# Sparse attention with a feed-forward block on one core: six early buffers for P, another set of numbers for the planner, and W2 loads and result stores issued by GpSimd

## The chip, the cores and the metric

The kernel runs on one NeuronCore of a Trainium2 chip. The metric is the device time of one execution in microseconds (us). Its engines are named as the profile names them: PE is TensorE (matmuls; PEld its weight loads), DVE is VectorE, ACT is ScalarE, POOL is GpSimd, SP is SyncE, which here only issues DMAs.

## The reference, cut to what matters

```python
# q, k, v: (4, 8, 768, 64) float32; blocks of 32 keys; 24 blocks
scores = (1/8) * q @ k.T
scores = where(mask, scores, -1e9)     # window, first/last block, 3 sampled blocks per query block
attn = exp(scores - max(scores)); attn = attn / (sum(attn) + 1e-9)
x = (attn @ v), heads side by side      # (4, 768, 512)
xn = (x - mean(x)) / sqrt(var(x) + 1e-6) * g_ln
out = x + relu(xn @ w_ch1) @ w_ch2      # 512 -> 2048 -> 512; w_ch1, w_ch2 are float64
```

## The kernel before, in words

The work is cut into 12 **units**, one for each batch and each chunk of 256 queries. A unit has 4 **segments**, one for each pair of heads, and a segment has 4 **slots** (2 tiles of 128 queries times 2 heads), 192 in all. Two slots make a pair, whose scores PE computes side by side, each head on 64 of the 128 rows.

All products are made of float16 halves. A number x is kept as a high part (x rounded to float16) and a low part (what is left), and a product is three matmuls: high times high, high times low, low times high. So queries, keys, values, P and both weight matrices are each split: somebody casts the high part (ACT by a cast, or a casting DMA that POOL issues), and DVE or POOL subtracts the low part.

For a slot PE makes the scores (`scores`, L587), DVE adds the mask and takes the maximum while it moves the scores from PSUM into P (`masked_max`, L596), ACT takes the exponential (L610). The first 9 segments are **early**: their P stays float32, PE transposes it (L625) into banks that ACT copies out (L632), and PE multiplies it with V in float32 (L701). Later segments split P into `ph` (ACT, L662) and `pl` (DVE, L666), and DMA transposes on SP's queue turn them.

After the 4 segments of a unit come the layer norm and the feed-forward block (`ffn`): 8 groups of the first product (FFN1, 24 matmuls each), each followed by ACT's high part `hh` (L883) and DVE's low part `hl` (L889), then the second product (FFN2) and the results `ot` (L905), which are stored to memory in 4 pieces per unit.

The weights come as float64 and are turned into scaled float32 by three integer steps on DVE (`first` L514, `second` L518, then `third` L522, or `third_low` L527 with an addition on POOL, L532, for those listed in `PORC`), cast to the high part on ACT (L556, L558; or by a DMA of POOL, L568, for those that are in both `HIDMA` and `PORC`), and the low part is subtracted by DVE (L564, those in `LOWDVE`) or POOL (L562). W1 comes in 8 pieces of 1 MB, W2 in 16 pieces of 0.5 MB. Their raw data use places that other data need as well: `raw0`, `raw1` (which the keys share) and unused parts of the weights' own tiles.

What sets the order is `Plan`: a list of tasks, each with an engine, a cost, tasks before it, a rank and buffers that it takes and gives back. `plan.run()` walks through them once when the program is built, picks on each engine the ready task with the earliest start, ties broken by rank, and emits instructions in this order. All engines then execute their own lists strictly in order, and wait only where data or buffers ask for it. So the numbers at the head of the function (ranks such as `W1AT`, `W2AT`, `AVAT`, `MASKAT`, offsets such as `EVAC`, `EXPO`) decide the order of every engine's list. Where the planner finds a hole on PE before `KEEP` nanoseconds, it puts in **filler** matmuls (L294), which compute nothing that is used.

Of the kernel before, what the change touches and what calls it, by code (L numbers as in the profile page):

```python
# [10 lines left out]
F16 = mybir.dt.float16  # L11
# [165 lines left out]
def sparse_attention_moe(  # L177
# [12 lines left out]
    nc = tc.nc  # L190
# [24 lines left out]
    SPLITAT = 7.38  # L215
    VDVE = 1
    KDVE, QDVE = 3, 1
    HIDMA = ((1, 5), (2, 15), (2, 2), (1, 7), (2, 5), (2, 4))
    LEAD = 2.8
    HIGHAT, LOWAT = -0.42, -1.36  # L220
    EVAC, EXPO = -9.12, 1.22
    PLAIN = 'full'
    LOWDVE = ((2, 12), (1, 3), (2, 2), (1, 6), (1, 1), (2, 8), (2, 11), (1, 7), (2, 4), (2, 15), (2, 6), (2, 3), (1, 0), (2, 13), (2, 5))
    AVHOLD = 4
    KEEP = 40000.0
    CASTK, CASTQ = 5, 6
    MASKAT = 25.07
    KAT, VAT, QAT = 11.39, 7.48, 12.65
    AVAT = -17.05
    W1AT = (8.87, 9.4, 10.72, 12.06, 12.3, 15.45, 16.92, 18.19)  # L230
    W2AT = (10.6, 14.04, 14.21, 15.7, 17.12, 20.44, 21.31, 22.16, 23.71, 24.25, 25.32, 25.67, 25.7, 25.75, 26.19, 28.74)
# [5 lines left out]
    pp = ctx.enter_context(tc.tile_pool(name="pp", bufs=2))  # L237
# [11 lines left out]

    plan = Plan()  # L250
# [33 lines left out]
    ql_s = [const.tile([P, CH], F16, name=f"ql{i}") for i in range(NQ)]  # L284
    w1h = const.tile([P, CT, DF], F16, name="w1h")
# [54 lines left out]
    def loads_k(b, pr, rank, before):  # L340
        idx = b * NPAIR + pr
        o = SimpleNamespace()

        def raw():
# [3 lines left out]
            nc.sync.dma_start(o.kr, ks[b, pr])  # L348
# [4 lines left out]
        o.raw = plan.add("SP", 580, raw, (before,), rank, 2000, load=1120, order="k",  # L353
# [773 lines left out]
```

## Time and profile before

| | |
|---|---|
| time, median of 3 runs | 793.22 us (792.82 to 796.02) |
| the profiled execution | 792.63 us, of which the span from first to last instruction is 790.9 us |
| granted TensorE clock | 0.999 of full speed |
| PE busy | 777.9 us (98%) |
| PEld, DVE, ACT, POOL busy | 599.3, 615.4, 498.3, 130.4 us |

The span is the time from the first to the last instruction of the profiled execution; the 1.7 us beside it lie before and after. A busy share is an average over the span.

### The profile page before, as it was taken

How to read it: one execution, taken by the hardware profiler on the slowest of the kernel's cores; microseconds unless marked ns; L12 is line 12 of the kernel's file. 1: busy time of each engine (PE TensorE's matmuls, PEld its weight loads, DVE VectorE, ACT ScalarE, POOL GpSimd, SP SyncE). 2: the span in 40 equal slices, each digit the busy share in tenths (PEclk: the TensorE clock that was granted, in tenths of full speed). 3: DMA queues.
4: the chain of work that ended last, by engine and by line, in shares of the span. 5: the costliest groups of instructions: out<-in, count | busy, mean ns of one | idle time of the engine just before them, and what ended most of it. 6: DMA issues, size and time to landing. Idle time of an engine off the chain costs nothing.

```text
span 790.9 us, 18452 instructions
## 1 busy us (share of the span) xinstructions
PE 777.9 (98%) x7327; PEld 599.3 (76%) x7327; DVE 615.4 (78%) x1216; ACT 498.3 (63%) x935; POOL 130.4 (16%) x140
## 2 busy tenths in 40 slices
PE   8999999999999999999999999999999999999998
PEld 5556677778777777777777777777777877778887
DVE  7999999979888778879877978778877878874220
ACT  6789776567676566667666667567656656652110
POOL 1343542321101002220101102120001100000000
PEclk9999999999999999999999999999999999999999
DMA  9463537998777567999667778997866755570000
GB/s 331 163 194 118 152 106 152 199 213 162 166 129 135 126 129 146 188 196 155 159 123 127 135 137 150 186 190 161 160 105 125 154 115 114 123 136 18 21 1 27
DMA packets 286694, 111.24 MB, mean 141 GB/s; under 512 B 253968, under 2 KB 278416, under 8 KB 286608
## 3 DMA queue, kind: packets, MB, share of 16 engines
q1 hardware_dynamic: 278544, 104.91, 61.2%
q0 software_dynamic: 7776, 5.05, 5.5%
q8 instruction: 57, 0.93, 0.5%
q14 instruction: 29, 0.24, 0.1%
q10 hardware_dynamic: 288, 0.10, 0.1%
HBM read 47.16 MB, written 6.29 MB: 68 GB/s over the span
## 4 chain that ended last, share of the span: by engine, by line
PE 88%; DVE 5%; ACT 3%; DMA 3%; issue 0%; ACTq 0%; DVEq 0%
PE bank L302 61%; PE ps L587 12%; PE pa L705 7%; PE pa L710 3%; PE pa L701 2%; PE bank L625 2%; DMA pt<-pl 2%; DVE p L596 1%; ACT p L610 1%; ACT pt L632 1%; DVE pl L666 1%; DVE allow L317 0%; DMA allow<-blocks 0%; PE pa L726 0%; PE bank L782 0%
## 5 line engine op out<-in xcount | busy, mean ns | idle before, releaser
L302 PE MATMUL bank<-hh,w2h 128*128 128x256 f16 x768 | 204.6, 273 | 0.0
L302 PE MATMUL bank<-hh,w2l 128*128 128x256 f16 x768 | 204.2, 273 | 0.0
L302 PE MATMUL bank<-hl,w2h 128*128 128x256 f16 x768 | 204.2, 273 | 0.0
L596 DVE CUSTOM_DVE_ANT_1 p<-ps,allow 128x768 f32<-128x768 f32 x192 | 178.1, 950 | 22.9 <-PE ps L587 22.6
L610 ACT ACTIVATE p<-p,st 128x768 f32<-128x768 f32 x192 | 178.4, 931 | 18.5 <-DVE st L596 18.2
L662 ACT ACTIVATE ph<-p,st 128x768 f16<-128x768 f32 x156 | 140.4, 927 | 59.6 <-DVE st L653 20.7
L666 DVE SCALAR_TENSOR_TENSOR pl<-p,st,ph 128x768 f16<-128x768 f32 x156 | 160.1, 1040 | 10.5 <-DMA pt<-pl 10.5
L302 PEld LDWEIGHTS <-w2h 128*128 128x128 f16 x1536 | 146.7, 98 | 27.0 <-issue 10.5
L302 PEld LDWEIGHTS <-w1h 128*128 128x128 f16 x1536 | 147.8, 98 | 25.5 <-issue 8.8
L302 PE MATMUL bank<-xh,w1h 128*128 128x256 f16 x768 | 115.4, 273 | 1.0 <-ACT pt L632 1.0
L302 PE MATMUL bank<-xh,w1l 128*128 128x256 f16 x768 | 115.4, 273 | 0.0
L302 PE MATMUL bank<-xl,w1h 128*128 128x256 f16 x768 | 115.4, 273 | 0.0
L889 DVE SCALAR_TENSOR_TENSOR hl<-bank,hh 128x512 f16<-128x512 f32 x96 | 66.1, 688 | 53.9 <-ACT hh L883 53.2
L883 ACT ACTIVATE hh<-bank 128x512 f16<-128x512 f32 x96 | 56.8, 591 | 75.3 <-PE bank L302 74.7
L302 PEld LDWEIGHTS <-w1l 128*128 128x128 f16 x768 | 73.8, 98 | 12.4 <-issue 4.1
L302 PEld LDWEIGHTS <-w2l 128*128 128x128 f16 x768 | 75.0, 98 | 9.1 <-issue 0.3
L705 PE MATMUL pa<-pt,vh 128*64 128x512 f16 x468 | 80.0, 383 | 0.9 <-DMA pt<-pl 0.9
L384 POOL DMA_DIRECT2D qh<-q x42 | 24.3, 579 | 277.7 <-PE ps L587 277.6
L587 PE MATMUL ps<-kh,qh 64*128 64x256 f16 (+1 forms) x384 | 66.0, 328 | 1.2 <-DVE st L596 1.1
L387 POOL TENSOR_TENSOR ql<-qr,qh 128x256 f16<-128x256 f32 x47 | 43.9, 935 | 139.9 <-DMA qr<-q 77.3
L587 PE MATMUL ps<-kl,qh 64*128 64x256 f16 (+1 forms) x384 | 64.4, 323 | 1.6 <-DVE kl L351 1.6
L587 PEld LDWEIGHTS <-qh 64*128 64x128 f16 x768 | 30.9, 94 | 45.8 <-issue 23.5
(110 smaller groups left out, 906.7 us busy)
## 6 DMA issues: line engine op xcount, KB each, us to landing
qr<-q SPq DMA_DIRECT2D x48, 128.0 KB, 2.8
raw<-k SPq DMA_DIRECT2D x16, 384.0 KB, 4.6
raw<-w SPq DMA_DIRECT2D x12, 512.0 KB, 3.9
vr<-v SPq DMA_DIRECT2D x32, 192.0 KB, 2.8
out<-ot SPq DMA_DIRECT2D x48, 128.0 KB, 1.9
w2l<-w SPq DMA_DIRECT2D x4, 1024.0 KB, 8.1
qh<-q POOLq DMA_DIRECT2D x42, 64.0 KB, 2.8
pt<-ph SPq DMA_TRANSPOSE x156, 2.7
```

What stands on the lines that cost most here:

```text
L302: nc.tensor.matmul(dst, w, x, start=start, stop=stop, skip_group_check=True)
L384: o.high = plan.add("POOL", 560, lambda: nc.gpsimd.dma_start(o.qh, qs[u.b, pr, u.c]), (o.raw,), rank, 2300, load=400, order="q")
L387: o.low = plan.add(e, x, lambda: (nc.vector if n < QDVE else nc.gpsimd).tensor_sub(o.ql, o.qr, o.qh), (o.raw, o.high), rank, give=(("qr", ...
L587: nc.tensor.matmul(s.ps[:, lo:hi], x[rows, s.qs], y[rows, lo:hi], start=n == 0, stop=n == len(terms) - 1)
L596: nc.vector.tensor_tensor_reduce(out=s.p.rearrange(blk, k=BLK), in0=s.ps[:, 0:S].rearrange(blk, k=BLK), in1=bias, scale=-0.125, scalar=3.0 ...
L610: nc.scalar.activation(s.p, s.p, AF.Exp, bias=s.st[:, j : j + 1], scale=-1.0, accum_out=total)
L662: nc.scalar.activation(s.ph, s.p, AF.Copy, scale=s.r)
L666: nc.vector.scalar_tensor_tensor(out=s.pl, in0=s.p, scalar=s.r, in1=s.ph, op0=ALU.mult, op1=ALU.subtract)
L705: nc.tensor.matmul(seg.pa[half[hh], 0 : 2 * CH], vo.vh[:, hh, t, :], pts[keys[hh]][:, t].rearrange("p i n -> p (i n)"), start=t == 0, stop ...
L710: nc.tensor.matmul(seg.pa[half[hh], 0:CH], vo.vl[:, hh, t, :], pts[keys[hh]][:, t, 0, :], start=False, stop=t == KT - 1, skip_group_check= ...
L883: nc.scalar.activation(u.hh[:, f : f + 2, :].rearrange("p f n -> p (f n)"), bank[plan.where("bank", own)], AF.Relu)
L889: nc.vector.scalar_tensor_tensor(out=u.hl[:, f : f + 2, :].rearrange("p f n -> p (f n)"), in0=bank[plan.where("bank", own)], scalar=0.0, i ...
```

## The change

P's buffers become fixed tiles. There are four float32 tiles, and the two tiles of 128x2x768 float16 that hold `ph` and `pl` later are used as a fifth and a sixth float32 P while the first 7 segments run. The first late segment's `ph` and `pl` wait for the transposes of these.

The first two segments make their scores from the raw float32 queries and keys (`RAWS_S` 2), one float32 product in place of three float16 ones. Keys 0 and 1 are split later all the same, for later units.

W2's 16 loads and the 48 stores of the result are issued by POOL instead of SP (`POOLQ`). ACT casts 14 of the 16 keys (5 before) and 10 queries (6 before); the casting DMAs of POOL for them go. DVE subtracts one key (`KDVE`) and one query (`QDVE`) more. The lists `PORC`, `HIDMA`, `LOWDVE` deal the steps of the weights out a little differently, and the ranks of W1 and W2 are lower, W2's far lower (4 to 10 in place of 11 to 29), which puts them ahead of scores of slots with a higher rank. Fillers are allowed up to 90 us in place of 40 us: there are 70 in place of 67.

```diff
-    EASY, EASE = 44, (249, 2530, 951)
-    PORC = ((2, 0), (2, 7), (1, 1), (2, 11), (2, 9), (1, 6), (2, 13), (2, 10), (1, 4), (2, 1), (2, 2))
+    EASY, EASE = 44, (85, 2529, 993)
+    PORC = ((2, 0), (2, 7), (1, 1), (2, 9), (1, 6), (2, 13), (2, 10), (1, 4), (2, 1), (1, 0))
...
-    RAWS_S = 0
+    RAWS_S = 2
...
-    KDVE, QDVE = 3, 1
-    HIDMA = ((1, 5), (2, 15), (2, 2), (1, 7), (2, 5), (2, 4))
+    KDVE, QDVE = 4, 4
+    HIDMA = ((1, 1), (1, 6), (2, 5), (2, 4), (2, 2), (1, 7), (1, 2))
+    POOLQ = ('o', 'w')
...
-    CASTK, CASTQ = 5, 6
+    CASTK, CASTQ = 14, 12
...
-    W2AT = (10.6, 14.04, 14.21, 15.7, 17.12, 20.44, 21.31, 22.16, 23.71, 24.25, 25.32, 25.67, 25.7, 25.75, 26.19, 28.74)
+    W2AT = (4.08, 5.97, 7.0, 7.03, 7.32, 7.48, 7.66, 8.54, 8.54, 8.94, 9.0, 9.05, 9.06, 9.08, 9.55, 9.62)
...
-    pp = ctx.enter_context(tc.tile_pool(name="pp", bufs=2))
...
+    def queue_of(kind):
+
+        return (nc.gpsimd, "POOL", 560) if kind in POOLQ else (nc.sync, "SP", 580)
+
...
+    plan.choice("p", range(6))
...
+    p_s = [const.tile([P, S], F32, name=f"p{i}") for i in range(4)]
+    halves_s = [const.tile([P, 2, S], F16, name=f"p{n}") for n in "hl"]
+    p_s += [x.rearrange("p i s -> p (i s)").bitcast(F32) for x in halves_s]
...
+        qw = "w" if kind == 2 else ""
...
-            nc.sync.dma_start(o.raw.rearrange("p e t -> p (e t)"),
+            queue_of(qw)[0].dma_start(o.raw.rearrange("p e t -> p (e t)"),
                               w2[i * P : (i + 1) * P, :].bitcast(I32))
...
     def masked_max(s):
-        s.p = pp.tile([P, S], F32, tag="p", name=f"p{s.i}", bufs=4)
+        s.p = p_s[plan.where("p", s.i)]
...
-            h = plan.add("ACT", 830, high, (inv,), r, 120, take=(("ph", s.i, 2),))
+            free = tuple(wides) if seg.i == EARLY else ()
+            h = plan.add("ACT", 830, high, (inv,) + free, r, 120, take=(("ph", s.i, 2),))
...
-            plan.add("SP", 580, lambda: nc.sync.dma_start(
+            plan.add(*queue_of("o")[1:], lambda: queue_of("o")[0].dma_start(
                 out[u.b, u.c, e * P : (e + 1) * P, :], u.outs[e]), (t,), -960, 1400, load=370,
                 give=(("ot", (i, e)),))
...
-                                  s.i, 160, take=(("p", s.i),), give=(("ps", s.i),), order="m")
+                                  s.i, 160, give=(("ps", s.i),), order="m",
+                                  take=(("p", s.i, 1, range(6 if seg.i < EARLY - 2 else 4)),))
```

How the lists of the engines move is shown at three places. The first is the start of DVE's list, from the first key's low part on. `ISA p` is a masked maximum (the `ISA st` behind it reads its accumulator), `kl0` and `kl1` are low parts of keys, `ql0` that of a query, `w1r0` the first piece of W1. Before:

```order
L351 TENSOR_TENSOR kl0_132<-raw0_118,kh0_131 128x768
L351 TENSOR_TENSOR kl1_138<-raw1_119,kh1_137 128x768
L596 ISA p0_217,st0_218<-ps0_198,allow_112 128x768
L596 ISA st0_218 128x1
L596 ISA p1_222,st0_218<-ps1_199,allow_112 128x768
L596 ISA st0_218 128x1
L514 TENSOR_SCALAR w2h_126<-w1r0_162 128x1024
L596 ISA p2_268,st2_269<-ps2_249,allow_112 128x768
```

And of the change:

```order
L360 TENSOR_TENSOR kl0_136<-raw0_115,kh0_135 128x768
L397 TENSOR_TENSOR ql0_117<-qr2_138,qh2_139 128x256
L608 ISA p0_121,st0_195<-ps0_179,allow_109 128x768
L608 ISA st0_195 128x1
L608 ISA p1_122,st0_195<-ps1_180,allow_109 128x768
L608 ISA st0_195 128x1
L360 TENSOR_TENSOR kl1_142<-raw1_116,kh1_141 128x768
L608 ISA p2_123,st2_232<-ps2_222,allow_109 128x768
L608 ISA st2_232 128x1
L608 ISA p3_124,st2_232<-ps3_223,allow_109 128x768
L608 ISA st2_232 128x1
L526 TENSOR_SCALAR w2h_129<-w1r0_185 128x1024
```

The first step of W1 stood behind two masked maxima and stands behind four, and the second key's low part moved from ahead of the first maximum to behind the second.

The second place is DVE's list where unit 0's first low part `hl0` (the one that gives back the bank of the first FFN1 group) stands. Before:

```order
L527 TENSOR_SCALAR raw1_119<-raw1_119 128x512
L514 TENSOR_SCALAR w2h_126<-w2h_126 128x512
L518 SCALAR_TENSOR_TENSOR w2h_126<-w2h_126 128x512
L889 SCALAR_TENSOR_TENSOR hl0_1104<-bank1_102,hh0_1099 128x512
L596 ISA p28_1108,st28_1109<-ps28_1085,allow_112 128x768
L596 ISA st28_1109 128x1
L596 ISA p29_1123,st28_1109<-ps29_1086,allow_112 128x768
```

And of the change:

```order
L526 TENSOR_SCALAR w2h_129<-w2h_129 128x512
L904 SCALAR_TENSOR_TENSOR hl0_996<-bank0_98,hh0_992 128x512
L608 ISA p2_123,st26_1006<-ps26_977,allow_109 128x768
L608 ISA st26_1006 128x1
L608 ISA p3_124,st26_1006<-ps27_978,allow_109 128x768
L608 ISA st26_1006 128x1
L530 SCALAR_TENSOR_TENSOR w2h_129<-w2h_129 128x512
L526 TENSOR_SCALAR w2l_130<-w2l_130 128x512
```

`hl0` stood ahead of slot 28's maximum and now stands ahead of slot 26's. On PE the first FFN1 group moved past the scores of slots 26 and 27 and 12 transposes in the same way.

The third place is POOL's list around the first pieces of W2 (`raw0`, `raw1`); `w1l` and `w1h` belong to W1's late pieces, `ql` are low parts of queries, a `DMA` row is a transfer that POOL issues. Before:

```order
L532 TENSOR_TENSOR w2h_126<-w2h_126,w2l_127 128x1024
L384 DMA qh9_862<-q 128x256
L387 TENSOR_TENSOR ql1_121<-qr9_861,qh9_862 128x256
L532 TENSOR_TENSOR raw0_118<-raw0_118 128x512
L384 DMA qh10_1039<-q 128x256
L532 TENSOR_TENSOR raw1_119<-raw1_119 128x512
L562 TENSOR_TENSOR w2l_127<-raw0_118,w2h_126 128x512
L562 TENSOR_TENSOR w2l_127<-raw1_119,w2h_126 128x512
L387 TENSOR_TENSOR ql2_122<-qr10_1038,qh10_1039 128x256
```

And of the change:

```order
L544 TENSOR_TENSOR w2h_129<-w2h_129,w2l_130 128x1024
L574 TENSOR_TENSOR w1l_128<-w2h_129,w1h_127 128x4x256
L580 DMA w1h_127<-w2h_129 128x4x256
L397 TENSOR_TENSOR ql3_120<-qr9_818,qh9_819 128x256
L515 DMA w2h_129<-w2 128x1024
L515 DMA w2l_130<-w2 128x1024
L544 TENSOR_TENSOR raw0_115<-raw0_115 128x512
L544 TENSOR_TENSOR raw1_116<-raw1_116 128x512
L574 TENSOR_TENSOR w2l_130<-raw0_115,w2h_129 128x512
L574 TENSOR_TENSOR w2l_130<-raw1_116,w2h_129 128x512
L515 DMA raw0_115<-w2 128x1024
L515 DMA raw1_116<-w2 128x1024
```

The loads of W2 stand in POOL's list now, the next load of `raw0` behind both additions and both subtractions, where it was on SP's queue and waited for its own subtraction only.

## Rows read from the trace of the kernel before

**Rows 1.** The page, part 1: busy time, share of the span and number of instructions of each engine.

```profile
PE 777.9 (98%) x7327; PEld 599.3 (76%) x7327; DVE 615.4 (78%) x1216; ACT 498.3 (63%) x935; POOL 130.4 (16%) x140
```

**Rows 2.** Busy time by stretch: start:end, length, busy us (and instructions) of PE, PEld, DVE, ACT, POOL, granted clock, DMA share, GB/s. The line at 84.82 ends where unit 0's first `hl` starts, that at 155.20 where its first result starts.

```profile
0.00:20.00 20.00, 17.07 (x131) 11.74 (x131) 14.27 (x30) 13.57 (x27) 2.94 (x9) 1.00 0.92 332
20.00:40.00 20.00, 17.93 (x156) 11.77 (x154) 19.78 (x35) 16.04 (x36) 7.31 (x6) 1.00 0.47 159
200.00:300.00 100.00, 100.00 (x967) 77.19 (x964) 79.92 (x161) 66.88 (x121) 10.83 (x14) 1.00 0.71 135
0.00:84.82 84.82, 76.93 (x641) 51.40 (x642) 76.78 (x138) 69.24 (x148) 30.39 (x30) 1.00 0.57 194
84.82:100.00 15.18, 14.38 (x134) 10.85 (x134) 14.10 (x31) 12.17 (x27) 7.19 (x7) 1.00 0.62 174
100.00:155.20 55.20, 54.97 (x512) 42.65 (x510) 51.77 (x107) 37.21 (x73) 18.84 (x17) 1.00 0.66 146
140.00:200.00 60.00, 59.15 (x562) 46.08 (x561) 52.80 (x106) 39.26 (x71) 14.79 (x16) 1.00 0.93 194
```

**Rows 3.** The waits of PE (three of its seven lines): who waited for whom, total us, times, longest.

```profile
PE bank L625 <- ACT pt L632: 2.3, 4, 0.9
PE ps L587 <- DVE kl L351: 1.6, 1, 1.6
PE pa L705 <- DMA pt<-pl: 0.9, 3, 0.4
```

**Rows 4.** DVE in order of time, from the start: start, us, instruction, and in brackets the idle time before it and who ended it.

```profile
3.43 0.43 DVE L387 TENSOR_TENSOR ql<-qr,qh 128x256 f16<-128x256 f32 x1 [2.28 <-ACT qh L382]
5.10 0.31 DVE L314 TENSOR_TENSOR w1h<-allow,samp_i 128x144 f32<-128x144 f32 x1 [1.25 <-DMA allow<-blocks]
6.70 2.29 DVE L351 TENSOR_TENSOR kl<-raw,kh 128x768 f16<-128x768 f32 x2
8.92 0.94 DVE L596 CUSTOM_DVE_ANT_1 p<-ps,allow 128x768 f32<-128x768 f32 x1
11.94 0.69 DVE L514 TENSOR_SCALAR w2h<-w1r 128x1024 int32<-128x1024 int32 x1 [1.20 <-DMA w1r<-w]
```

**Rows 5.** PE in order of time around the first FFN1 group: a score pair, transposes, and the group's end.

```profile
78.48 0.39 PE L587 MATMUL ps<-kh,qh 64*128 64x512 f16 x2
79.56 0.44 PE L625 MATMUL bank<-ident,p 128*128 128x128 f32 x2
79.83 0.60 PE L302 MATMUL bank<-xh,w1h 128*128 128x256 f16 x4
82.70 0.87 PE L625 MATMUL bank<-ident,p 128*128 128x128 f32 x6
83.51 0.39 PE L587 MATMUL ps<-kh,qh 64*128 64x512 f16 x2
85.62 0.60 PE L302 MATMUL bank<-xh,w1h 128*128 128x256 f16 x4 [0.96 <-ACT pt L632]
```

**Rows 6.** Groups of instructions by line: count, busy us, mean ns of one, idle before them.

```profile
L596 DVE CUSTOM_DVE_ANT_1 p<-ps,allow 128x768 f32<-128x768 f32 x192 | 178.1, 950 | 22.9 <-PE ps L587 22.6
L351 DVE TENSOR_TENSOR kl<-raw,kh 128x768 f16<-128x768 f32 x3 | 3.2, 1104 | 0.0
L387 DVE TENSOR_TENSOR ql<-qr,qh 128x256 f16<-128x256 f32 x1 | 0.4, 426 | 2.3 <-ACT qh L382 2.3
L522 DVE SCALAR_TENSOR_TENSOR w2h<-w1r,w2h 128x1024 int32<-128x1024 int32 x1 | 1.2, 1219 | 0.0
L527 DVE TENSOR_SCALAR w1r<-w1r 128x1024 int32<-128x1024 int32 x1 | 1.0, 994 | 0.0
L532 POOL TENSOR_TENSOR raw<-raw 128x512 int32<-128x512 int32 x6 | 9.4, 1566 | 23.7 <-DVE raw L527 22.4 <-DMA vr<-v 1.2
L562 POOL TENSOR_TENSOR w2l<-raw,w2h 128x512 f16<-128x512 f32 x5 | 6.5, 1305 | 2.3 <-ACT w2h L556 2.3
L294 PE MATMUL bank<-ones,ones_h 128*128 128x256 f16 x67 | 9.7, 307 | 1.2 <-DVE eps L272 1.2
```

**Rows 7.** One piece of the chain that ended last: start, us, what; 8 records of float32 matmuls, four of 256 columns.

```profile
67.28 1.92 PE bank L782 x8
```

**Rows 8.** POOL's casting DMAs of queries (duration of the issue on POOL), and DMA issues: KB each and median us from issue to landing.

```profile
L384 POOL DMA_DIRECT2D qh<-q x42: 567/567/765, 32.0 to 643.4; - x42
raw<-w SPq DMA_DIRECT2D x12, 512.0 KB, 3.9
out<-ot SPq DMA_DIRECT2D x48, 128.0 KB, 1.9
qh<-q POOLq DMA_DIRECT2D x42, 64.0 KB, 2.8
w2h<-w2h POOLq DMA_DIRECT2D x1, 128.0 KB, 2.5
```

**Rows 9.** DVE in order of time: a step of W1 that lay beside one of POOL's DMA issues (at 67.16 us), and a step of W2.

```profile
66.66 1.11 DVE L514 TENSOR_SCALAR w2h<-w2h 128x1024 int32<-128x1024 int32 x1
83.17 1.67 DVE L518 SCALAR_TENSOR_TENSOR w2h<-w2h 128x512 int32<-128x512 int32 x1
```

**Rows 10.** The end: the last result on DVE and its store on SP's queue.

```profile
787.48 0.42 DVE L905 SCALAR_TENSOR_TENSOR ot<-bank,xT 128x256 f32<-128x256 f32 x1 [4.82 <-PE bank L302]
787.93 0.33 SPq L911 DMA_DIRECT2D out<-ot  x1
```

More of the change, by code (lines that the diff above doesn't have):

```diff
@@ L360, in loads_k @@
             o.high = plan.add("POOL", 560, lambda: nc.gpsimd.dma_start(o.kh, ks[b, pr]),
-                              (o.raw,), rank, 2300, load=1100, order="k")
+                              (o.raw,), rank, 2300, load=1500, order="k")
         e, x = ("DVE", 870) if idx < KDVE else ("POOL", 1640)
@@ L374, in raw @@
                 o.ql = ql_s[plan.where("q", n)]
-            nc.sync.dma_start(o.qr, qs[u.b, pr, u.c])
-        o.raw = plan.add("SP", 580, raw, (before,), rank, 2000, load=370, order="q",
+            queue_of(qk)[0].dma_start(o.qr, qs[u.b, pr, u.c])
+        o.raw = plan.add(*queue_of(qk)[1:], raw, (before,), rank, 2000, load=370, order="q",
                          take=(("q", n), ("qr", n)) if n >= RAWS_S else (("qr", n),))
@@ L384, in loads_q @@
             o.high = plan.add("POOL", 560, lambda: nc.gpsimd.dma_start(o.qh, qs[u.b, pr, u.c]),
-                              (o.raw,), rank, 2300, load=400, order="q")
+                              (o.raw,), rank, 2300, load=600, order="q")
         e, x = ("DVE", 345) if n < QDVE else ("POOL", 660)
@@ L455, in raw @@
                     dst = o.vr[j] = rawp.tile([P, KT, D], F32, tag="vr", name=f"vr{o.idx}_{j}")
-                nc.sync.dma_start(dst.rearrange("p t d -> p (t d)"), v[b, 2 * pr + j])
+                queue_of(qv)[0].dma_start(dst.rearrange("p t d -> p (t d)"), v[b, 2 * pr + j])
             take = (() if early else (("vr", (o.idx, j)),)) + ((("v", o.idx),) if j == 0 else ())
-            o.last = plan.add("SP", 580, raw, (o.last,), rank, 2000, load=550, take=take, order="v")
+            o.last = plan.add(*queue_of(qv)[1:], raw, (o.last,), rank, 2000, load=550, take=take, order="v")
             o.raw.append(o.last)
@@ L536, in loads_w @@
             after += tuple(low_tail)
-        ld = plan.add("SP", 580, load, after if kind == 1 or i >= 10 else after + tuple(
+        ld = plan.add(*queue_of(qw)[1:], load, after if kind == 1 or i >= 10 else after + tuple(
             w1done if not low_tail and i > 1 else ()), rank - LEAD, 2000,
@@ L568, in loads_w @@
             o.high = plan.add("POOL", 560, lambda: nc.gpsimd.dma_start(o.dh, o.src), (d,), rank + HIGHAT,
[L569 removed]
+                              2300, load=2270 * size)
         else:
@@ L637, in attention_early @@
                 take = (("pt", key),) if s.t == 0 and part == 0 else ()
+                if part and seg.i < EARLY - 2:
+                    wides.append(x)
                 y = plan.add("DVE" if dve else "ACT", 335 if dve else (470, 300)[part], out_,
@@ L659, in high @@
             def high(s=s):
-                s.ph = pp.tile([P, S], F16, tag="ph", name=f"ph{s.i}")
+                s.ph = halves_s[0][:, plan.where("ph", s.i)]
                 s.r = s.st[:, 4 + s.h % 2 : 5 + s.h % 2]
```

40 lines of the change are left out of this document (21 added, 19 removed).

## The prediction

> **What bounds the kernel now.** I began with the busy times of the whole span [rows 1]: PE 98%, and no other engine over 78%. A busy PE need not be a PE that gets on, so I read the stretches next [rows 2]. From 200 to 300 us PE is busy all the time, while DVE has a fifth and ACT a third of it free. There only less work on PE could help, and the change takes none away. The start is another matter: in the first 20 us PE has 17.07, from 20 to 40 us 17.93, and there DVE has 19.78 of 20. Until unit 0's feed-forward block gives PE something that it can always do, PE follows DVE, which has masked maxima and the conversion of W1 and W2 to do. From 100 us to 155.2 us PE has 54.97 of 55.20. So what the change can win or lose is decided ahead of about 100 us, and at the very end.
>
> The waits of PE say the same in small [rows 3]: a few us in all, on ACT's copies and one low part of a key. That list is short because PE's own lists are full of short blocks and fillers (67 filler matmuls, 9.7 us, [rows 6]), so I don't take the list as the whole loss. The measure I use is DVE: up to unit 0's first `hl`, at 84.82 us, it is busy 76.78 us and idle 8.0 [rows 2]. Of these 8.0, 3.5 are the waits for the first query's cast and for the mask, and 1.2 the wait for the first piece of W1 [rows 4].
>
> **The change, part by part.** The sum is made for the profiled execution, 792.63 us; the median of the runs shown is 0.6 higher.
>
> *DVE up to the first `hl`.* Counting DVE's list up to that instruction in both programs, the change has two masked maxima less (slots 26 and 27 come later), one `third` of 1024 columns and one W2 `second` less, one `third_low`, one key and one query more. By [rows 6, 9]: two maxima, less the 0.07 by which neighbours overlap, -2 x 0.88; `third` -1.14 (1.22 less overlap); the `second` -1.1 (between 0.6, which it usually costs, and the 1.67 of the one in rows 9); `third_low` +0.93; the key's low part +1.03; the query's +0.43. Sum -1.6 us.
>
> *The wait for W1.* In the new order the first step of W1 stands behind four maxima and not two, so two more maxima and a key's low part are done in the 1.2 us in which DVE waited [rows 4]. I take the wait as gone: -1.2. If W1's load, which has one load of V more ahead of it, lands a microsecond later, half of it stays: the range of this term is -1.2 to 0. The first maximum itself comes hardly sooner, since the mask's data still end DVE's wait at 5.10 [rows 4].
>
> So the first `hl` should come 2.8 us sooner.
>
> *What PE has left at this point.* FFN1 moved ahead of the scores of slots 26 and 27 and of 12 transposes. These are now behind it: a pair of scores takes 1.08 us (78.48 to 79.56) and six transposes 0.81 [rows 5], so +2.7. The two terms nearly cancel: -0.1.
>
> *From there to 100 us.* PE is idle 0.8 of 15.18 us, and once waits 0.96 for a bank [rows 2, 5]. In the new list the second to fourth `hl` stand 1.7 to 4.2 us of DVE work sooner, so FFN1 is there to fill these holes: -0.8, bounds -1.5 and 0.
>
> *Raw float32 scores.* Four pairs. A float32 matmul of 256 columns takes 0.48 us (four in 1.92, [rows 7]), so 768 columns 1.44 if the two heads run side by side, against 1.08: +0.36 each, +1.4. These pairs lie where fillers lie [rows 6] and where two maxima of DVE take 1.8 us, which hides them: 0. If the heads don't run side by side, a pair takes 2.9 and up to 1.1 each is seen: bound +4.4. Pairs of float16 matmuls start together in [rows 5] (x2 in 0.39), so I take 0. Six buffers for P by themselves cost and win nothing here: none of DVE's waits in [rows 4], nor PE's in [rows 3], names a full P.
>
> *Keys on ACT.* Nine more casts of keys and four of queries, spread over the whole span, on an engine that has 37% free [rows 1]: 0.
>
> *140 to 200 us.* The DMA engines are 93% busy there and PE misses 0.85 us, with three waits for transposed P [rows 2, 3]. W2 is loaded sooner and the keys are not read twice: -0.5, bounds -0.9 and 0.
>
> *POOL as issuer.* An issue took 0.57 us at the median and 0.77 at most [rows 8]. A step of DVE beside one took 1.11 us [rows 9], 0.4 more than its 0.7 elsewhere. Sixteen loads of W2, of which one in six or so meets such a step: 3 x 0.4 = +1.2, part of it off the path; I take +0.5, bounds 0 and +1.2. The Trainium skill (SBUF — State Buffer, 🔬 SBUF: two separate sides) warns of more: while DVE runs an operation that holds the port pair it shares with GpSimd, GpSimd can't write the descriptors of a DMA that it issues, and the same page advises SP or ACT as the issuer. The rows here agree that the two hinder each other, but by tenths: 42 issues between 0.57 and 0.77. By that rule, with each load held for a whole step of up to 1.1 us, the loads would come some 18 us later in all, a rival below.
>
> *The end.* The last store leaves SP at 787.93, right behind the last result [rows 10], and nothing hides it. Stores from SP land after 1.9 us, POOL's DMAs after 2.5 and 2.8 [rows 8]: +0.6 to +0.9, I take +0.7.
>
> Sum: -0.1 - 0.8 + 0 - 0.5 + 0.5 + 0.7 = -0.2 us. With the bounds it goes from -1.9 to +7.6 (all bad ends at once, 4.4 of it the serial scores). On the good side I lean a little further than -0.2: DVE's idle time ahead of the first `hl` still holds about 2 us of short waits that I counted as unchanged, and with more conversion steps ready sooner some of them should close. I take -1.0: 792.63 + 0.6 - 1.0, so **792.2 us**.
>
> **Rivals.**
>
> *The early stage closes up.* If the weights, being ahead in the lists, leave DVE no hole at all, its idle time up to unit 0's first result, 155.20 - 142.65 = 12.5 us [rows 2], shrinks to the start's 4.8 (the waits until 5.10, [rows 4]). DVE's list up to there is 1.8 us longer (the key, the query, a masked maximum more, less a `pl`), and the work that PE has left at that point is the same. So -7.7 + 1.8 = -5.9, and the end +0.7: 788.0. For it: DVE is nearly full anyway. Against: DVE's waits for PE's scores don't go away by conversions that other waits hold up. 0.27.
>
> *POOL holds up W2 or W1 (slower).* Now POOL's list feeds the conversion: the load that refills `raw0` stands behind two additions of 1.57 and two subtractions of 1.3 [rows 6], then 3.9 us to land [rows 8], 9.6 in all, while DVE in between has some 8.6 us of listed work (five maxima, 5 x 0.88, and steps of 0.4 to 0.7). So the first refill is already late by a microsecond unless DVE is idle by as much, and each later refill that isn't covered shows its issue and landing, 0.57 + 3.9 = 4.5 us. In the same way one of W1's low parts on DVE now waits for a casting DMA of POOL, with unit 0's layer norm queued behind it. Before, SP issued these loads with only its own buffer to wait for. PE would have slots' scores and FFN1 to do meanwhile, but these hang on DVE too. Two uncovered refills: +9 - 1 = 8 more, 801. It decides from the point where POOL is a further 3 us behind. 0.13.
>
> *DVE holds POOL's issues.* If each load of W2 is held for a whole step of DVE of 1.11 us [rows 9], POOL gives away 16 x 1.1 = 18 us, of which DVE's list sees what isn't covered; with half of it, +9: 802. Against it stand all 42 issues of [rows 8]. 0.04. This is what the rule of the Trainium skill's page on SBUF, named above, would do here.
>
> *Nothing of either kind*, the sum above: 0.56.
>
> **Numbers.** A change under 0.5% (4 us) can't be told from none for this kernel. The likeliest case lies within 789 and 796; the range takes in most of the first rival and the milder half of the second: 787.5 to 797. Faster by over 0.5% (under 789.3) is the first rival and a little of the main case, 0.29; slower (over 797.2) the second and third, 0.15; the same 0.56.
>
> **What would show it.** In the changed kernel's trace: DVE's wait for `w1r` gone; the first `hl` at 82.0 us; DVE's busy time up to there 75.1; no wait of DVE on W2's loads over 1 us; PE busy in all but 0.5 us from 85 to 100; POOL's issues at 0.57 us; the span's end 0.7 us later behind the last result than before. Wrong would be: a wait of DVE on a `raw` load or on `w1h` of several us (second rival), issues of POOL over 1 us (third), or PE full from 70 us on (first).

## The result and the profile after

The changed kernel takes 800.42 us (median of 5 runs, 799.27 to 802.39) where the kernel before takes 793.22 (5 runs): a ratio of 1.0078, 95% interval 1.0062 to 1.0094, 7.2 us more by the medians. The prediction said 792.2 and 787.5 to 797.0. It was wrong, on the slow side. One execution of all those below, 891.04 us in experiment 15, lay far above the others of its kernel and is left out of the ratio there.

The profiled execution of the changed kernel took 802.39 us, its span is 800.6. Busy times are hardly other than in [rows 1]:

```profile
PE 781.2 (98%) x7314; PEld 602.6 (75%) x7314; DVE 612.5 (77%) x1217; ACT 507.0 (63%) x949; POOL 148.9 (19%) x186
```

So the time is not in any engine's work. I looked for it in the stretches of [rows 2], with the same columns (start:end, length, busy us and count of PE, PEld, DVE, ACT, POOL, granted clock, DMA share, GB/s); unit 0's first `hl` starts at 83.20 here, its first result at 156.01.

```profile
0.00:83.19 83.19, 77.46 (x599) 50.20 (x600) 70.65 (x134) 63.55 (x138) 29.73 (x28) 1.00 0.59 198
83.19:100.00 16.81, 16.81 (x156) 13.55 (x158) 16.54 (x34) 14.03 (x32) 6.20 (x9) 1.00 0.60 190
100.00:156.01 56.01, 54.86 (x515) 42.82 (x515) 51.90 (x107) 42.12 (x84) 21.37 (x23) 1.00 0.54 122
140.00:200.00 60.00, 56.98 (x535) 46.32 (x534) 49.99 (x97) 38.49 (x68) 13.73 (x17) 1.00 0.89 171
200.00:300.00 100.00, 100.00 (x967) 76.05 (x966) 84.53 (x170) 69.30 (x127) 13.17 (x21) 1.00 0.74 146
791.00:800.60 9.60, 0.00 (x0) 0.00 (x0) 0.00 (x0) 0.00 (x0) 0.27 (x1) 0.73 0.04 14
```

Up to the first `hl` 1.6 us are won, PE is full from there to 100 us, between 140 and 200 us PE misses 3.0 us where it missed 0.85, and from 200 us on it is full as before. The last row is the surprise: in the last 9.6 us of the span no engine computes anything. In order of time, the last result on DVE, and its store, which POOL issues:

```profile
790.01 0.42 DVE L920 SCALAR_TENSOR_TENSOR ot<-bank,xT 128x256 f32<-128x256 f32 x1 [4.82 <-PE bank L310]
790.73 0.54 POOL L926 DMA_DIRECT2D out<-ot  x1 [4.70 <-DVE ot L920]
```

From the start of the last result to the end of the span there are 10.6 us; in [rows 10], with a span of 790.9, 3.4. That is 7.2 us, the whole difference of the medians. (The two profiled executions differ by 9.7 us; the other 2.5 lie ahead of the last result, and this execution was the slowest of the five.) What fills them stands in no list of busy times. The chain that ended last breaks off with a piece of 0.56 us on POOL's sequencer at the program's closing line, L1137:

```profile
786.03 4.68 issue
790.71 0.56 POOLq L1137
```

The view of that source line alone (duration in ns: least, median, longest; first and last start in us) tells more:

```profile
L1137 POOLq DRAIN  x3: 46/102/9131, 790.7 to 800.3; - x3
```

POOL ends its program with an instruction called DRAIN, which here starts with the last store and lasts 9.13 us. The data of that store land long before it ends: in the trace the last packet of POOL's queue is over at 792.36. In the kernel before the same line reads:

```profile
L1121 POOLq DRAIN  x3: 40/93/5202, 645.9 to 790.6; - x3
```

It was there too, 5.20 us long, but at 645.9 us: POOL's list ended with the last query, and the DRAIN lay beside 140 us of other work.

### The profile page after: what moved, and what is told of

Its sections match the earlier page's. It is cut to its first block, busy times and chain, and to the rows that moved or that the text cites. A ratio compares the mean times of both kernels' runs of the same rounds, so it can differ in the third digit from the quotient of the medians.

```text
span 800.6 us, 18438 instructions
## 1 busy us (share of the span) xinstructions
PE 781.2 (98%) x7314; PEld 602.6 (75%) x7314; DVE 612.5 (77%) x1217; ACT 507.0 (63%) x949; POOL 148.9 (19%) x186
## 4 chain that ended last, share of the span: by engine, by line
PE 84%; issue 7%; DMA 3%; DVE 2%; ACT 2%; POOL 1%; SPq 0%; POOLq 0%; DVEq 0%
PE bank L310 55%; PE ps L599 13%; PE pa L720 7%; PE pa L725 3%; PE pa L716 3%; PE bank L637 2%; PE bank L302 1%; ACT pt L644 1%; DMA pt<-pl 1%; DMA raw<-w 1%; DVE p L608 1%; DMA out<-ot 1%; DMA raw<-k 1%; POOL out L926 0%; PE pa L741 0%
## 5 line engine op out<-in xcount | busy, mean ns | idle before, releaser
L608 DVE CUSTOM_DVE_ANT_1 p<-ps,allow 128x768 f32<-128x768 f32 x184 | 170.3, 951 | 24.5 <-PE ps L599 24.2
L622 ACT ACTIVATE p<-p,st 128x768 f32<-128x768 f32 x184 | 170.6, 929 | 14.0 <-DVE st L608 14.0
L926 POOL DMA_DIRECT2D out<-ot x48 | 26.7, 556 | 302.2 <-DVE ot L920 280.3
L725 PE MATMUL pa<-pt,vl 128*64 128x256 f16 x468 | 65.9, 273 | 0.0
L599 PE MATMUL ps<-kh,qh 64*128 64x512 f16 (+1 forms) x368 | 62.2, 328 | 0.4 <-DVE st L608 0.4
L599 PE MATMUL ps<-kl,qh 64*128 64x512 f16 (+1 forms) x368 | 61.0, 323 | 0.0
L599 PE MATMUL ps<-kh,ql 64*128 64x512 f16 (+1 forms) x368 | 60.7, 322 | 0.0
```

What stands on the lines that cost most here:

```text
L599: nc.tensor.matmul(s.ps[:, lo:hi], x[rows, s.qs], y[rows, lo:hi], start=n == 0, stop=n == len(terms) - 1)
L608: nc.vector.tensor_tensor_reduce(out=s.p.rearrange(blk, k=BLK), in0=s.ps[:, 0:S].rearrange(blk, k=BLK), in1=bias, scale=-0.125, scalar=3.0 ...
L622: nc.scalar.activation(s.p, s.p, AF.Exp, bias=s.st[:, j : j + 1], scale=-1.0, accum_out=total)
L725: nc.tensor.matmul(seg.pa[half[hh], 0:CH], vo.vl[:, hh, t, :], pts[keys[hh]][:, t, 0, :], start=False, stop=t == KT - 1, skip_group_check= ...
L926: plan.add(*queue_of("o")[1:], lambda: queue_of("o")[0].dma_start(out[u.b, u.c, e * P : (e + 1) * P, :], u.outs[e]), (t,), -960, 1400, loa ...
```

## The experiments

All times are medians; a ratio is to the kernel before, run on the same chip in turn. Experiments were run on four chips, where the kernel before took 793.7 to 794.8 us, so times of different experiments are compared by their ratios. "The changed kernel" has the ratio 1.0078.

**1. The last unit's stores back on SP** (`e1_after_tail_sp`).

```diff
-            plan.add(*queue_of("o")[1:], lambda: queue_of("o")[0].dma_start(
+            qo = "o" if i < len(units) - 1 else ""
+            plan.add(*queue_of(qo)[1:], lambda: queue_of(qo)[0].dma_start(
```

> The changed kernel with one edit: the four stores of the last unit go back to SP; all other stores and W2 stay with POOL, and no other instruction moves. Theory (closing wait of POOL): in the changed kernel 9.9 us lie between the issue of the last store (790.73) and the end of the span (800.6), in the kernel before 3.0 (787.93 to 790.9); 6.9 us go, so some 793.5 us against 800.4, within 0.3% of the kernel before, and POOL's closing instruction is short. Rival (stores and W2 through POOL are late all along the program, and the tail only shows it): nothing but POOL's own store latency goes, some 0.7 us, so 799.7.

Measured: 792.95 us, ratio 0.9987 (0.9972 to 1.0002). The end of it, on DVE, then SP's queue, then the closing line:

```profile
788.61 0.43 DVE L920 SCALAR_TENSOR_TENSOR ot<-bank,xT 128x256 f32<-128x256 f32 x1 [4.82 <-PE bank L310]
```

```profile
789.06 0.33 SPq L927 DMA_DIRECT2D out<-ot  x1
```

```profile
L1138 POOLq DRAIN  x3: 46/93/8805, 747.4 to 791.5; - x3
```

The DRAIN is not short, as I had expected, but 8.81 us long; only it begins with the store of the unit before, at 747.4, where nobody waits for it. From the last result to the span's end (791.7) it is 3.1 us. Four stores of 48 are the whole loss: 1.0078 - 0.9987 is 0.9%, 7.2 us. The rival is out.

**2 and 3. One store of the kernel before on POOL** (`e2_before_last_pool`, `e3_before_third_pool`): the last one, or the one ahead of it.

```diff
-            plan.add("SP", 580, lambda: nc.sync.dma_start(
+            q, name, cost = (nc.gpsimd, "POOL", 560) if (i, e) == (len(units) - 1, CT - 1) else (nc.sync, "SP", 580)
+            plan.add(name, cost, lambda: q.dma_start(
```

> The kernel before with one edit: its very last store is issued by POOL in place of SP. Theory (closing wait of POOL, set by how late its last transfer is issued, not by how many it issued): 6.9 us more, 800.1 us, with a closing instruction on POOL of some 9 us. Rival (the closing wait grows with the number of POOL's transfers of the whole program or of the W2 and result bytes through POOL): the single store costs what its longer landing costs, 2.6 against 1.9 us, so 793.9.

> The kernel before with one edit: the store ahead of the last one is issued by POOL, the last by SP. The two are 5.24 us apart (782.24 and 787.48 for the tiles). Theory (POOL's closing wait runs for a set time from its last transfer's issue): POOL would be done 9.9 us after an issue at 782.7, at 792.6 in place of 790.9, so 1.7 us more, 794.9. Rival (it is the wait for the landing of data alone, or begins only when all the other engines are done): landed data cost nothing, 793.2; begun at the end it would cost the whole 6.9, 800.1.

Measured: the last one, 796.93 us, ratio 1.0040 (1.0027 to 1.0054); the one ahead of it, 794.02 us, ratio 1.0004 (0.9987 to 1.0020). Closing line of the first:

```profile
L1122 POOLq DRAIN  x3: 46/93/5166, 788.6 to 794.3; - x3
```

One store costs 3.2 us, neither the 6.9 nor the longer landing alone (0.7). The place matters as the theory says (the same DRAIN of 5.17 us, begun at 784.3 in the second kernel, is free), but the length was not a set time: 5.17 and not 9.13.

**4. All stores on SP** (`e4_after_out_sp`).

```diff
-    POOLQ = ('o', 'w')
+    POOLQ = ('w',)
```

> The changed kernel with all 48 stores of the result issued by SP, W2 still by POOL (the planner lays out its order anew from the first store on, at about 155 us). Theory (only the end matters): the same as with the last four stores on SP, 793.5, within 1 us. Rival (POOL's stores also hold up tiles of the result, raw keys or the splits on POOL in the steady part): 1 to 3 us below that, 790.5 to 792.5. A third way: SP's queue fills with stores and the transposes of P come later, 1 to 3 us above.

Measured: 793.55 us, ratio 0.9994 (0.9982 to 1.0006). The same as experiment 1: POOL's stores cost nothing except at the end.

**5 and 6. The last two, or four, stores of the kernel before on POOL** (`e5_before_last2_pool`, `e6_before_last4_pool`); the condition of experiment 2 becomes, for four (for two, with `and e >= CT - 2`):

```diff
+            q, name, cost = (nc.gpsimd, "POOL", 560) if i == len(units) - 1 else (nc.sync, "SP", 580)
```

> The kernel before with its last two stores issued by POOL. With the last one alone POOL's closing instruction took 5.17 us and the kernel 796.9; in the changed kernel, with four stores 5.24 us apart, it took 9.13. Theory (it pays for each transfer that POOL issued shortly before the end, some 1.3 us apiece): 6.5 us, 798.2. Rival 1 (one transfer shortly before the last is enough for the full length): 9.1 us, 800.8. Rival 2 (the length has nothing to do with the last stores, but with how much POOL issued in the program): 5.2 us, 796.9.

> The kernel before with the four stores of the last unit issued by POOL, as at the end of the changed kernel. Theory (per recent transfer) and rival 1 (one neighbour is enough): a closing instruction of 9.1 us and 800.8. Rival 2 (the whole program's count): 5.2 us and 796.9.

Measured: 797.90 us, ratio 1.0041 (1.0029 to 1.0053), and 798.05, ratio 1.0046 (1.0034 to 1.0058). The closing lines read 5214 and 5369 ns, and the ratios are near that of the single store (1.0040), so what I called the theory fell, and rival 2 holds: the last stores don't set the length. Now I counted what POOL had issued in each program (in the changed kernel 48 stores, 36 and 2 casts of queries and keys, 16 loads of W2, 2 casts of W1: 104):

| kernel | transfers issued by POOL | closing DRAIN, us |
|---|---|---|
| before | 54 | 5.20 |
| experiments 2, 3 | 55 | 5.17 |
| experiments 5 and 4 | 56 | 5.21, 5.41 |
| experiment 6 | 58 | 5.37 |
| experiment 10 (below) | 84 | 7.50 |
| experiment 1 | 100 | 8.81 |
| changed kernel | 104 | 9.13 |

A line through 55 and 104 transfers, (9.13 - 5.17) / 49 = 0.081 us for each transfer and 0.73 besides, goes through the rest to 0.2 us. Bytes don't set the length: 56 transfers of 11.67 MB in all (experiment 4) gave 5.41 us, 84 of 9.05 MB (experiment 10) 7.50.

**7. All stores on POOL in the kernel before** (`e9_before_all_out_pool`), a forecast by that line.

```diff
-            plan.add("SP", 580, lambda: nc.sync.dma_start(
+            plan.add("SP", 580, lambda: nc.gpsimd.dma_start(
                 out[u.b, u.c, e * P : (e + 1) * P, :], u.outs[e]), (t,), -960, 1400, load=370,
```

> The kernel before with all 48 stores issued by POOL at their old places in the order; the lists of PE, DVE and ACT stay word for word. Counted over the profiles so far, POOL's closing instruction took 5.17 us after 55 transfers issued by POOL in the whole program, 5.21 after 56, 5.37 after 58, 7.50 after 84, 8.80 after 100 and 9.13 after 104: a line of 0.73 us plus 0.081 us for each. Theory (that line, whatever the transfers carry): 54 + 48 = 102 give 9.0 us, and since this stands behind the last result, 7.0 us more than before (the last store alone, with 55, cost 3.2): a ratio of 1.0088 to the kernel before, some 801. Rival (the length follows the bytes that POOL moved, 5.2 to 18.0 MB, or W2's loads): 5.2 MB plus 6.3 for the stores lies near the 11.7 and 9.1 MB that gave 5.4 and 7.5, so at most 7.5 us, a ratio of 1.007 or less.

Measured: 800.54 us, ratio 1.0084 (1.0068 to 1.0100):

```profile
L1121 POOLq DRAIN  x3: 46/93/8961, 787.8 to 797.3; - x3
```

8.96 us against a forecast of 9.0. So the kernel before, with no other change than the issuer of its stores, is as slow as the changed one.

**8 and 9. Still more transfers on POOL** (`f2_after_v_pool`, 24 loads of V; `f3_after_q_pool`, 40 loads of queries; one execution each). In `loads_v`, and in the same way in `loads_q` for `n >= 8`:

```diff
-                queue_of(qv)[0].dma_start(dst.rearrange("p t d -> p (t d)"), v[b, 2 * pr + j])
+                (nc.gpsimd if b else nc.sync).dma_start(dst.rearrange("p t d -> p (t d)"), v[b, 2 * pr + j])
```

> The changed kernel with 24 loads of V issued by POOL in place of SP, at their places in the order: 128 transfers by POOL, the last of them the last store. If the line goes on, POOL's closing instruction takes 0.73 + 128 x 0.081 = 11.1 us and the kernel 802.5. If it begins anew past some number (115 gave 3.79 us, as 38 would, 77 less), 128 gives 0.73 + 51 x 0.081 = 4.9 us and the kernel 796.3.

> The changed kernel with 40 loads of queries issued by POOL in place of SP: 144 transfers by POOL. If the line goes on: 0.73 + 144 x 0.081 = 12.4 us and 803.8. If it begins anew and the 77 hold: 0.73 + 67 x 0.081 = 6.2 us and 797.6. If the 115 was something else, neither.

Measured: 793.75 and 794.96 us. The closing line of the first:

```profile
L1137 POOLq DRAIN  x3: 51/102/3150, 788.0 to 791.7; - x3
```

The second has 4.15 us. Neither forecast came in. Past 104 transfers the line no longer holds; if the count starts anew, it is not at a fixed number: by the line 3.15, 4.15 and the 3.79 us of experiment 14 answer to 30, 42 and 38 transfers, which leaves 98, 102 and 77 ahead of them. Whether it starts anew, and what makes it, stays open. These two kernels keep the last stores on POOL, and their tails are 4.6 and 5.6 us for it.

**10. W2 on SP** (`e7_tail_sp_w2_sp`): experiment 1, and in `load` for W2:

```diff
-            queue_of(qw)[0].dma_start(o.raw.rearrange("p e t -> p (e t)"),
+            nc.sync.dma_start(o.raw.rearrange("p e t -> p (e t)"),
```

> The changed kernel with the last unit's stores on SP (792.95) and one edit more: the sixteen W2 loads are issued by SP at the same place of the planned order, so that the lists of PE, DVE and ACT stay word for word. Theory (POOL as the issuer costs nothing, since DVE waited for a raw W2 tile 0.6 us at most): 793.0, within 0.5. Rival 1 (POOL's loads come late and their landing of 4.5 us against 3.9 delays the second unit): up to 2 us less, 791. Rival 2 (the loads hold up the transposes of P behind them on SP, each load waiting for its raw buffer): 1 to 3 us more, 794 to 796.

Measured: 793.11 us, ratio 0.9982 (0.9973 to 0.9992), against 0.9987: no difference. POOL's issues of W2 and of the results in the changed kernel (ns: least, median, longest):

```profile
L515 POOL DMA_DIRECT2D raw<-w x12: 528/531/573, 57.3 to 140.3; - x12
L926 POOL DMA_DIRECT2D out<-ot x48: 540/550/584, 156.7 to 790.7; - x48
```

None is held up. This version has the lowest ratio of all that were run, by its interval a little faster than the kernel before; with six more fillers (experiment 16) that is gone, so it may be chance.

**11. Without float32 scores** (`e8_tail_sp_no_f32_scores`): experiment 1, and the line below; the planner lays the order out anew.

```diff
-    RAWS_S = 2
+    RAWS_S = 0
```

> The changed kernel with the last unit's stores on SP (792.95) and without the scores in float32 of the first two pairs of heads: their keys and queries are split as in the kernel before, and the planner lays out the order anew. Theory 1 (the shorter list of DVE is worth more than the slow passes cost): the first FFN1 tile of hl comes 1.6 to 2.8 us later, 794.5 to 795.7. Theory 2 (the float32 passes, 8.3 us for four pairs where three float16 terms take about 1 us a pair, are what keeps the start from closing up): 1.5 to 2 us sooner, 791 to 791.5. Between them, within 0.5 us of 793.0, both would be paid for by work that PE has to fill anyway.

Measured: 795.35 us, ratio 1.0009 (0.9999 to 1.0020), 0.2 to 0.3% above experiments 1 and 10, some 2 us. The interval lies above that of experiment 10 and overlaps that of experiment 1. That is theory 1's size; its way can't be told from one profile: the first `hl` stands at 82.9, against 81.4 in experiment 1 and 83.2 in experiment 10. With an order laid out anew around them, the float32 scores are worth about 2 us by the times; where, one profile doesn't show.

**12. Four buffers for P** (`e10_tail_sp_four_p`): experiment 1, and:

```diff
-                                  take=(("p", s.i, 1, range(6 if seg.i < EARLY - 2 else 4)),))
+                                  take=(("p", s.i, 1, range(4)),))
```

> The changed kernel with the last unit's stores on SP (0.9987 of the kernel before) and four buffers for P all along, as before; the order of the lists stays. Theory (the prediction: no wait names a full P): no difference, 0.9987, some 793. Rival (with four, maxima wait for the transposes of the P two pairs back, and everything up to the first hl comes later): 1 to 3 us more, up to 1.0025, with waits of DVE on PE's transposes in the first 80 us.

Measured: 793.89 us, ratio 0.9998 (0.9988 to 1.0009); the interval overlaps that of experiment 1, and the first `hl` stands at 81.2 against 81.4. No effect that can be told.

**13. W2's due times as before** (`e11_tail_sp_w2_late`): experiment 1, with the old numbers:

```diff
-    LEAD = -1.09
+    LEAD = 2.8
...
-    W2AT = (4.08, 5.97, 7.0, 7.03, 7.32, 7.48, 7.66, 8.54, 8.54, 8.94, 9.0, 9.05, 9.06, 9.08, 9.55, 9.62)
+    W2AT = (10.6, 14.04, 14.21, 15.7, 17.12, 20.44, 21.31, 22.16, 23.71, 24.25, 25.32, 25.67, 25.7, 25.75, 26.19, 28.74)
```

> The changed kernel with the last unit's stores on SP (0.9987 of the kernel before) and the due times of W2 and the lead of its loads as before; up to 120 us DVE's list hardly changes, from there the maxima of the second unit stand ahead of steps of W2 again. Theory 1 (W2 ahead delays the second unit's scores and P, the transposed P is late by 3.0 us against 0.9): 2 us less, 0.996, some 791, and PE's waits for transposed P under 1 us. Theory 2 (what W2 gains in the first unit's second matrix it gives back in the second unit, and PE has work either way): within 0.7 us of 0.9987. Theory 3 (the rest of the order is laid out for W2 early): 1 us more or worse.

Measured: 794.94 us, ratio 1.0013 (1.0001 to 1.0024): theory 3, some 2 us worse by the ratios, though the interval just touches that of experiment 1. PE's waits for transposed P fall only from 3.3 to 2.4 us, and unit 0's first result comes at 158.0, 4 us later. So W2 ahead of the second unit's scores, with the lead of its loads, is worth some 2 us in this order, and most of the late P has another cause.

**14. Casts of keys and queries as before** (`e12_tail_sp_keys_dma`): experiment 1, and:

```diff
-    CASTK, CASTQ = 14, 12
+    CASTK, CASTQ = 5, 6
```

> The changed kernel with the last unit's stores on SP (0.9987 of the kernel before) and the casts of keys and queries as before: from the sixth key and the seventh query on by casting transfers of POOL, laid out anew by the planner. Theory (the prediction: casts on ACT are hidden and cost nothing): within 0.7 us of 0.9987, with DMA busier between 140 and 200 us. Rival 1 (the second read of the keys delays the transposes of P): 1 to 2 us more. Rival 2 (ACT's casts hold up its copies and exponents): 1 us less.

Measured: 799.97 us, ratio 1.0073 (1.0053 to 1.0093), outside all three. The first `hl` comes at 94.7 and not 81.4: the planner's new order puts 13.6 us more of DVE's work ahead of it (84.24 us busy up to there, against 70.61). This run prices another order, not the casts.

**15 and 16. The start** (`f1_tail_sp_more_fillers`, experiment 1 with 24 fillers in place of 18 ahead of the first scores, and `f4_tail_w2_sp_more_fillers`, the same on experiment 10). PE in order of time in the changed kernel, and in experiment 1, whose lists are the same there:

```profile
1.20 4.02 PE L302 MATMUL bank<-ones,ones_h 128*128 128x256 f16 x18 [1.20 <-DVE eps L277]
5.91 2.93 PE L599 MATMUL ps<-raw,qr 64*128 64x512 f32 x8 [0.69 <-DMA raw<-k]
8.78 2.96 PE L302 MATMUL bank<-ones,ones_h 128*128 128x256 f16 x19
```

```profile
1.20 3.77 PE L302 MATMUL bank<-ones,ones_h 128*128 128x256 f16 x18 [1.20 <-DVE eps L277]
6.13 1.56 PE L599 MATMUL ps<-raw,qr 64*128 64x512 f32 x8 [1.16 <-DMA raw<-k]
7.62 2.25 PE L302 MATMUL bank<-ones,ones_h 128*128 128x256 f16 x19
```

The same eight float32 matmuls take 2.93 or 1.56 us from one execution to the next. In the kernel before PE had 26 fillers there, up to 5.8 us.

```diff
-            self.filler(place, count)
+            self.filler(place, count + (0 if self.work else 6))
```

> The changed kernel with the last unit's stores on SP (0.9987 of the kernel before) and six more fillers of PE ahead of the first scores (24 in place of 18), which at 0.21 us each end at about 6.1 us in place of 4.8; no other list changes. Theory (PE comes to its full rate, fillers of 0.11 us in place of 0.21, by 5.7 us if it goes on working; with the gap from 4.8 on it stays slow, in some executions until 10 us): the first float32 pair takes 1.56 us, the first maximum of the second pair stands at 11.0 to 11.6, and the executions with a slow start gain 1.9 us: a ratio of 0.9975, some 791.9. Rival (the slow first pair has nothing to do with the gap): the fillers only stand in the pair's way by 0.3 us, 0.999, and first pairs of 2.93 us still occur.

> The version that the runs so far point to: the changed kernel with the last unit's stores and all of W2's loads on SP (0.9982 of the kernel before) and six more fillers of PE ahead of the first scores. Theory (the gap in PE's work keeps it slow at the start in some executions): 0.9970, and the first float32 pair takes 1.56 us. Rival (the gap is not the cause): 0.998 to 0.9985.

Measured: 793.81 us, ratio 0.9993 (0.9977 to 1.0008), and 792.98, ratio 0.9995 (0.9984 to 1.0006). PE in the first of them:

```profile
1.20 5.30 PE L302 MATMUL bank<-ones,ones_h 128*128 128x256 f16 x24 [1.20 <-DVE eps L277]
6.43 1.66 PE L599 MATMUL ps<-raw,qr 64*128 64x512 f32 x8
```

In both profiles the pair is short (1.66 and 1.87 us), but it starts 0.3 to 0.6 us later, and the ratios don't fall. As a gain it failed, and the mechanism isn't shown either: without the extra fillers the pair took 1.56 us in five of nine profiled executions, so two short pairs of two can be chance. The theory had the fillers fall from 0.21 to 0.11 us each by 5.7 us if PE goes on working; in both profiles PE worked on from 1.2 us, and the filler that starts at 5.9 still took 0.21.

## Why the prediction was wrong, step by step

**The end** is the step that failed: +0.7 us, bounds 0.6 and 0.9, and it measured 7.2. I priced the landing of a transfer (1.9 us from SP against 2.5 to 2.8 from POOL; in the trace of after 2.6 at the median, though the last store itself took 2.0 against 1.7 in the kernel before), which was near enough and beside the point. What lies at the end is not the store but what its issuer does after its last instruction. The row was to be had: POOL's closing DRAIN of 5.20 us in the kernel before, hidden at 645.9 us. I had read [rows 10], where the span ends 3 us behind SP's store, and took these 3 us as given for any issuer. No rival had this mechanism; the second and third came near its time (801 and 802) by ways that didn't happen.

**Everything but the end** was forecast at -1.7 us (792.2 less its 0.7, against 793.2). Experiment 1 leaves only the end out and measures -1.0 us (0.9987; -2.2 to +0.2). As a sum this held, though no change at all lies in the interval too. Its terms did less well:

- *DVE up to the first `hl`*: -1.6 forecast, busy time measured 70.65 against 76.78, -6.1. The count was right; but steps were also shorter, by 4.5 us in all, and 2.5 of these stand in the steps of the mask, before and after (count, busy us, mean ns, idle before):

```profile
L317 DVE TENSOR_TENSOR allow<-allow,w1h 128x48 f32<-128x48 f32 (+1 forms) x6 | 3.9, 642 | 0.2
```

```profile
L325 DVE TENSOR_TENSOR allow<-allow,w1h 128x48 f32<-128x48 f32 (+1 forms) x6 | 1.4, 233 | 0.2
```

- What lay beside them differs. Three of these steps and an addition of POOL in the kernel before, then the same three steps in the changed kernel, where POOL has nothing to do from 1.3 to 21.6 us:

```profile
24.35 3.30 DVE L317 TENSOR_TENSOR allow<-allow,w1h 128x96 f32<-128x96 f32 x3
24.82 2.42 POOL L532 TENSOR_TENSOR w2h<-w2h,w1r 128x1024 int32<-128x1024 int32 x1
```

```profile
16.11 0.84 DVE L325 TENSOR_TENSOR allow<-allow,w1h 128x96 f32<-128x96 f32 x3
```

- One of the three took 2.35 us in the kernel before and ended 0.1 us behind the addition; alone such a step takes 0.26. It seems that the changed order won some of its time by moving DVE's steps away from POOL's, which the sum has no term for. This is read from the times of one trace each; no run tests it. Against it DVE's idle time there rose from 8.0 to 12.5 us (10.8 in experiment 1), so the lean of 0.8 us on closing waits had no ground.
- *The wait for W1* is gone, as said; what came in its place are waits for PE's first scores (in brackets), which [rows 4] didn't have:

```profile
8.85 0.96 DVE L608 CUSTOM_DVE_ANT_1 p<-ps,allow 128x768 f32<-128x768 f32 x1 [0.89 <-PE ps L599]
13.26 0.96 DVE L608 CUSTOM_DVE_ANT_1 p<-ps,allow 128x768 f32<-128x768 f32 x1 [1.70 <-PE ps L599]
15.02 0.69 DVE L526 TENSOR_SCALAR w2h<-w1r 128x1024 int32<-128x1024 int32 x1
83.20 0.69 DVE L904 SCALAR_TENSOR_TENSOR hl<-bank,hh 128x512 f16<-128x512 f32 x1 [0.78 <-ACT hh L898]
```

- *The first `hl`* at 82.0: 83.2 in this profile, 81.0 to 82.4 in experiments 1, 8, 9, 12, 13, 15 and 16, whose first score pair was faster. Right within what one execution differs from the next.
- *85 to 100 us*: PE idle at most 0.5. It is idle 0.0. Right.
- *Float32 scores* at 0: the later pairs take 1.56 to 1.95 us, so near the 1.44 for two heads side by side, and not the 2.9 of the bound, but the first pair does take 2.93 in some executions. Experiment 11 makes the whole item a gain of some 2 us. Undersized, and in the other direction than its bound.
- *140 to 200 us* at -0.5, not above 0: PE misses 3.0 us where it missed 0.85, so +2.2. All of it stands in PE's waits (who waited for whom: us, times, longest):

```profile
PE pa L720 <- DMA pt<-pl: 3.0, 3, 1.9
```

- I had argued with less to transfer, and there is a little less (DMA share 0.89 against 0.93). By the order of time P was made late by DVE and ACT: unit 1's last layer-norm step starts at 145.3 in place of 140.6, and SP's queue has no transpose to issue from 144 to 149 us. Which of the new numbers sets this is open: with W2's old ranks 2.4 us of these waits stay (experiment 13), with the old casts the list of waits has none (experiment 14), but that is another order from the start.
- *POOL as issuer* at +0.5: 0 (experiments 4 and 10). DVE waited for W2's raw data 0.6 us in all. So the second rival is refuted. The third also: the Trainium skill (SBUF — State Buffer, 🔬 SBUF: two separate sides) would have POOL's issues held for as long as DVE has the port pair, and POOL's 16 loads of W2 took 0.53 to 0.57 us each beside a DVE that was busy nine tenths of the time. What looks like this hold stands in other traces, by tenths. In experiment 14 two loads of W2 took 0.76 us, and each ended 0.12 us behind a DVE step (first load, DVE's step):

```profile
93.49 0.76 POOL L515 DMA_DIRECT2D raw<-w  x1 [3.41 <-DVE raw L534]
93.72 0.41 DVE L526 TENSOR_SCALAR w2h<-w2h 128x512 int32<-128x512 int32 x1
```

- The +0.5 rested on a misread row besides. The step of 1.11 us in [rows 9] lay beside an addition of POOL (from 64.80 to 67.21) before it lay beside an issue. A step beside little but an issue took its usual 0.69, and there the issue was the one that took longer:

```profile
53.14 0.69 DVE L514 TENSOR_SCALAR w2h<-w2l 128x1024 int32<-128x1024 int32 x1
53.19 0.77 POOL L384 DMA_DIRECT2D qh<-q  x1
```

- The sign of the third rival, an issue over 1 us, did appear once in the trace of after: 1.10 us at 66.6, but for a cast of W1, not a load of W2.
- *Keys on ACT* and *six P* at 0: the second agrees with experiment 12; the first was not isolated.

The first rival, an early stage that closes up, didn't come: PE still misses 5.7 of the first 83 us, and DVE's idle time up to unit 0's first result went from 12.5 us to 16.9 (156.01 - 70.65 - 16.54 - 51.90). Its 4.8 us of waits at the start should have read 4.4, which puts it at 787.6 in place of 788.0 and changes nothing.

## What to carry to other kernels

Before a last store is moved to another issuer, look at what each engine does after its last instruction, by the program's closing source line: a time that is hidden in the middle of a kernel becomes part of it when it moves to the end. If GpSimd issues transfers, let its last one be some 10 us ahead of the end (the closing instruction took 9.13 us at most here) and give the final stores to another queue; here four stores were worth 7.2 us. And where a sum of small terms comes out near zero, the ends of the program deserve a row of their own, since nothing hides there.

## What the runs showed of the hardware

- POOL's closing DRAIN lasts 0.73 us plus 0.081 us for each transfer that POOL issued in the whole program (54 to 104 transfers, 5.2 to 9.1 us), whatever they carry and however long ago most of them landed. With 115, 128 and 144 transfers it was 3.8, 3.2 and 4.1 us; why is open.
- The page of the profile hides it: it counts in no engine's busy time, and the chain shows 0.56 us of it.
- DVE and POOL can take longer beside each other. A mask step of DVE took 2.35 us beside an addition of POOL and 0.26 alone; a load that POOL issues took 0.76 us in place of 0.53 and ended 0.12 us behind a step of DVE. This is read from times in the traces; no run was made to test it.
- The first matmuls of the program run at about half the rate of later ones (experiment 13: 18 fillers in 4.02 us, 19 in 2.25 later on), although the granted clock reads 1.00, the 2.4 GHz level, in the whole stretch. After a gap of 0.5 to 1.2 us in PE's work, until the keys came at 5.4 to 6.3 us, the first float32 pair took 2.93 us in some executions and 1.56 in others. In the changed kernel with 2.93 the second pair starts 1.9 us and the first `hl` 1.8 us later than in experiment 1 with 1.56. What decides between the two is open.
